# Reordered first loads, pre-gated down weights, a DMA-transposed norm and a new instruction order in an adaLN transformer block

## The chip, the cores and the metric

The kernel runs on one core of one Trainium2 chip. The metric is the device time of one execution in microseconds (us). A run counts as slow when it is over 1.5% above the fastest of the same kernel. The granted clock is TensorE's clock as a share of its full speed; over a stretch it is a mean. Engines are called TensorE (PE in the profile), VectorE (DVE), ScalarE (ACT), GpSimd (POOL) and SyncE (SP), the last of which issues nearly all DMAs here.

## The reference, cut to what matters

A block with adaptive layer norm: 2048 tokens, width 448, 16 heads of 28, a dilated local window of 8 keys (distance 2), and a gated feed-forward part with 1792 hidden columns.

```python
mod = (silu(c) @ w_mod).reshape(...)           # six rows of 448: sa, ca, ga, sb, cb, gb
h = layernorm(x) * (1 + ca) + sa
x = x + ga * attention(h, A_wqkv, A_wo)        # local window, 8 keys
h = layernorm(x) * (1 + cb) + sb
gate = h @ W_gate; up = h @ W_up
h = relu(gate) * up
x = x + gb * (h @ W_down)
```

## The kernel before

The kernel records some 900 operations with their dependencies, estimated costs and priorities. A list scheduler in the kernel's own Python then fixes, before anything is compiled, the order of instructions on every engine. Tokens are handled in four blocks of 512 (b = 0 to 3), in tiles of 128. hT is the normalized block, transposed; the V projection makes v from it and the QK projections make q and k. PSUM is the memory that TensorE writes (psF and psL in the profile), and an eviction copies a result out of it. The parts that the change and the argument touch:

```python
# first loads: x tiles 0-1 and then c on ScalarE's queue, the rest on SyncE's
load_x(0, 2, -9, eng=ACTE)
load(crow[:], c..., ["crow"], 4096, -9, eng=ACTE)
for i, (k0, k1) in enumerate(PARTS_A):
    load(wmod[...], ["wmodA" + str(i)], ...)       # modulation weights for the first norm
    if i == 0:
        load_x(2, 4, -8)
...
load(Wd[:], B_W_down..., [("Wd", f) ...], FF * D * 2, -1)   # 1.57 MB, last of the loads

# first norm of a block by TensorE: normalize -> 16 transposes into PSUM ->
# four evictions that apply scale and shift (two on ScalarE, two on VectorE)
def stage_a_pe(b, prio, groups): ...
# the same by GpSimd and DMA transposes; in the source before, but used for no block (DMAT = ())
def stage_a_dma(b, prio, groups): ...

# output tile of the down stage: PSUM * gate, + x, store
def stage_out(t, buf, eng, eprio):
    o = _Buf(o_slots)
    op(DVE, 620, ... o = buf * gbc[:, 1, :])
    op(eng, ..., ... o = o + x_sb[:, t, :])        # VectorE in the last block, else GpSimd
    op(SP, 0, ... store o)
```

The softmax here doesn't subtract the row's maximum and nothing guards it: scores larger than these inputs give would overflow.

Of the kernel before, what the change touches and what calls it, by code (L numbers as in the profile page):

```python
# [6 lines left out]
ALU = mybir.AluOpType  # L7
# [3 lines left out]
D = 448  # L11
# [4 lines left out]
NF = FF // 128  # L16
NB = 4
# [6 lines left out]
EPS = 1e-5  # L24
DN64 = (1, 2)
PR = {
    "ln1": [537, 334, 2613, 2241],
    "qk": [711, 1230, 2349, 2507],
    "qke": [2263, 2215, -826, -631],
    "v": [2180, 2636, 348, 408, 1319, 433, 2040, 2244, -1257],  # L30
    "at": [374, 331, 536, 709, -821, 2168, 1026, -349, -365, 591, 241, 236, 1043, 1920, 2533, -19, 2605, 2025],
    "ae": [-692, 650, -783, 337, -1128, -747, 13, -538, 1769, -29, 6, 739, 473, 2242, 453, 1030, -831, 2496],
    "y": [-360, 506, 1780, 457, 2055, -380, 840, 939],
    "ye": [2666, -18, 1084, 2214, 693, 151, -437, 215],
    "ln2": [2233, 536, -825, 351],
    "gu": [562, 2728, -159, 2532],
    "dn": [882, 2869, 674, 2816],
    "ffe": [331, 1314, 632, 2250],
    "misc": [2507, 2310, 2251, 237],
}  # L40
T32 = 5
DMAT = ()
SWAP_DVE = (0,)
ACT_TABLE_LN_EXP = 6

# [21 lines left out]


class _Plan:
    SWITCH = 105.0  # L70
    XLAT = 95.0
    DMA_FIXED = 2000.0
    DMA_NS_PER_BYTE = 1.0 / 255.0

# [40 lines left out]
    def schedule(self):  # L115
# [39 lines left out]
        for _ in range(n):  # L155
            cands = {e: [] for e in ENGINES}
            for oid in avail:
                o = ops[oid]
                slot_t = 0.0
                bad = False  # L160
                taken = set()
                for b in o["allocs"]:
                    s = slot_for(b, taken)
                    if s is None:
                        bad = True
                        break
                    taken.add((id(b.slots), s[1]))
                    slot_t = max(slot_t, s[0])
                if bad:
                    continue  # L170
                best = None
                for a, (e, c, f) in enumerate(o["alts"]):
                    rt = slot_t
                    for d in o["deps"]:
                        if d in o["after"]:
                            t = finish[d] + 40.0
                        elif e == PE and who[d] == PE:
                            t = finish[d] - ops[d]["drain"]
                        else:
                            t = finish[d] + lat(d, e)  # L180
                        if t > rt:
                            rt = t
                    st = max(free[e] + (self.SWITCH if e == PE and o["mode"] != mode else 0.0), rt)
                    if e == DVE and o["port"]:
                        st = max(st, free[POOL])
                    elif e == POOL and not o["dma"] and port is not None:
                        st = max(st, finish[port])
                    if best is None or st + c < best[0] - 1e-6:
                        best = (st + c, st, a, e)
                cands[best[3]].append((best[1], o["prio"], oid, best[2]))  # L190
            pick = None
            for e in ENGINES:
                cl = cands[e]
                if not cl:
                    continue
                tmin = min(c[0] for c in cl)
                sel = min((c for c in cl if c[0] <= tmin + slack[e]), key=lambda c: (c[1], c[2]))
                if pick is None or sel[0] < pick[0]:
                    pick = (sel[0], e, sel[2], sel[3])
            if pick is None:  # L200
                raise RuntimeError("static scheduler: dependency cycle")
            st, e, oid, a = pick
            o = ops[oid]
            o["eng"], cost, o["fn"] = o["alts"][a]
            for b in o["allocs"]:
                t, i = slot_for(b)
                prev = b.slots.last[i]
                if prev is not None:
                    o["deps"].update(prev.users)
                b.slots.last[i] = b  # L210
                b.i = i
            if o["dma"]:
                free[e] = st + o["issue"]
                b0 = max(free[e], dma_free)
                dma_free = b0 + o["dma"] * self.DMA_NS_PER_BYTE
                finish[oid] = dma_free + self.DMA_FIXED
            else:
                free[e] = st + cost
                finish[oid] = free[e] + o["drain"]
                if e == POOL and port is not None:  # L220
                    o["deps"].add(port)
                if e == DVE and o["port"]:
                    port = oid
            o["st"] = st
            if e == PE:
                mode = o["mode"]
            who[oid] = e
            order[e].append(oid)
            commit.append(oid)
            avail.remove(oid)  # L230
            for s in succ[oid]:
                left[s] -= 1
                if left[s] == 0:
                    avail.append(s)
# [61 lines left out]


def _mm(n):
    return max(n, 60) / 2.4 + 3.0


def _act(n, ptr=0):
# [3 lines left out]
def _dve(n, per=1.04, fixed=150.0, ptr=0):  # L306
    return fixed + per * n + 90.0 * ptr


PE_DRAIN = 175.0  # L310


def bass_adaLN_cond__sliding_local_dilated__glu_gated_reglu__prompt_kernel(
# [15 lines left out]
    with ExitStack() as es:  # L329
# [121 lines left out]

        PARTS_A = ((0, 2), (2, 3), (3, 4))
        wmod_v = w_mod.rearrange("(p k) n -> p k n", k=4)
        load_x(0, 2, -9, eng=ACTE)
        load(crow[:], c.rearrange("o (p k) -> (o p) k", k=4), ["crow"], 4096, -9, eng=ACTE)
        for i, (k0, k1) in enumerate(PARTS_A):
            load(wmod[0:112, k0:k1, 0:2 * D], wmod_v[:, k0:k1, 0:2 * D], ["wmodA" + str(i)], (k1 - k0) * D * D, -8)
            if i == 0:
                load_x(2, 4, -8)
        load(Wv[:, 0:3, :], A_wqkv[0:384, 2 * D:3 * D].rearrange("(k p) n -> p k n", p=128),  # L460
# [138 lines left out]
        def stage_a_pe(b, prio, groups):  # L599
# [21 lines left out]
            for j in range(4):  # L621
                hbufs.append(ln_normalize(t0 + j, rstd, nmr, 1, prio, ((0, 1), (0, 1, 2), (2,), (2,))[b]))
                if b == 0:
                    op(PE, 4 * 64, lambda e, j=j: tr(e, (j,)), r=[hbufs[j], "ident"], w=pairs[2 * (j // 2):2 * (j // 2) + 2] + [("tr", b, j)], prio=prio,
                       drain=PE_DRAIN)
                    if j < 3:
                        keep_busy(1, prio, 300, [("tr", b, j)])
            if b:
                op(PE, 16 * 64, lambda e: tr(e, range(4)), r=hbufs + ["ident"], w=pairs + [("tr", b, 3)], prio=prio,
                   drain=PE_DRAIN)  # L630
            for h in range(1 if b else 2):
                for cc in range(4):
# [253 lines left out]
                   r=[bufs[1], gs] + ([hh] if f else []), w=[(hh, f)] + ([] if f else [hh] + extra), prio=eprio)  # L886
            return hh

        def stage_out(t, buf, eng, eprio):
            o = _Buf(o_slots)  # L890
            op(DVE, 620, lambda e: e.tensor_tensor(o.at, buf.at[:, 0:D], gbc[:, 1, :], ALU.mult), r=[buf, ("gbc", 1)], w=[o],  # L891
               prio=eprio)
            op(eng, 400 if eng == DVE else 1030, lambda e: e.tensor_tensor(o.at, o.at, x_sb[:, t, :], ALU.add), r=[o, ("x", t)],  # L893
               w=[(o, "x")], prio=eprio, port=eng == DVE)
            op(SP, 0, lambda e: e.dma_start(out2d[128 * t:128 * t + 128, :], o.at), r=[o, (o, "x")], w=[("out", t)], prio=0,
               dma=128 * D * 2)
# [25 lines left out]

        def stage_down1(b, hh, prio, eprio):
            for j in range(4):
                buf = _Buf(poolF if b == NB - 1 else poolM)
                for part in range(2):
                    def mm(e, j=j, buf=buf, part=part):
                        last = None
                        for f in range(7 * part, 7 * part + 7):
                            last = e.matmul(buf.at[:, 0:D], hh.at[:, f, 128 * j:128 * j + 128], Wd[:, f, :],  # L930
                                            start=(f == 0), stop=(f == NF - 1))
                        return last
                    op(PE, 7 * _mm(D), mm, r=[hh] + [(hh, f) for f in range(7 * part, 7 * part + 7)] +
                       [("Wd", f) for f in range(7 * part, 7 * part + 7)], w=[buf], prio=prio, drain=PE_DRAIN)
                t = 4 * b + j
                stage_out(t, buf, DVE if b == NB - 1 else POOL, eprio)


        mod_cols((0, 1), "wmodA", 0, -5, PARTS_A)
# [28 lines left out]
        for t in range(NA):  # L968
            stage_attn(t, PR["at"][t], PR["ae"][t])
            end = sum(span(t)[:2])  # L970
            while done_y < NT and 128 * (done_y + 2) <= end:
                stage_y(done_y, PR["y"][done_y // 2], PR["ye"][done_y // 2])
                done_y += 2
                if done_y % 4 == 0:
                    h2s.append(stage_ln2(done_y // 4 - 1, PR["ln2"][done_y // 4 - 1]))
        for b in range(NB):
            hh = stage_gu(b, h2s[b], PR["gu"][b], PR["ffe"][b])
            (stage_down if b in DN64 else stage_down1)(b, hh, PR["dn"][b], PR["ffe"][b])

# [53 lines left out]
```

## Time and profile before

224.74 us (median of 3 runs, 224.7 to 225.2). The first lines of the page of the kernel before: span, busy time with its share and the number of instructions, then the busy tenths in 40 slices of 5.6 us.

```profile
span 222.2 us, 5740 instructions
PE 212.7 (96%) x2452; PEld 102.7 (46%) x2452; DVE 143.3 (65%) x299; ACT 119.5 (54%) x210; POOL 49.1 (22%) x73
...
PE   7699999989999999999999999999999999999992
...
DVE  2889999888879967842387659569444304544251
ACT  2658799989879697340286676822333301433200
POOL 7402450310220020028302001281660005100000
...
DMA  6999999900130030021302000240440001100011
```

TensorE is busy nearly everywhere, but "busy" hides slow stretches: until about the tenth slice VectorE and ScalarE are nearly full as well, because they empty PSUM for TensorE and run the softmax. Loads fill the DMA engines through the eighth slice. Waits, by stretch and by engine (each line of waits: who waited for whom, us in total, times, longest; the stretch line: length, then busy us of TensorE, its weight loads, VectorE, ScalarE, GpSimd, then granted clock, DMA share, GB/s):

```profile
ACT cexp L490 <- DMA crow<-in_c_dram: 4.9, 1, 4.9
PE psF L507 <- DVE silu L493: 1.7, 1, 1.7
```

```profile
30.00:40.00 10.00, 9.56 (x178) 4.86 (x175) 9.70 (x20) 9.73 (x17) 1.71 (x3) 1.00 1.04 231
```

The time can be cut into three pieces at two landmarks: the start of the first V projection (the first useful large matmul) and the first matmul of the last down stage. The timeline of the kernel before (start, length, what, count):

```profile
11.58 3.30 PE L724 MATMUL psF<-Wv,hT 64*128 64x448 bf16 x28
...
217.89 0.62 DVE L891 TENSOR_TENSOR o_sb<-psF,gbc 128x448 bf16<-128x448 f32 x1 [1.53 <-PE psF L930]
218.55 0.39 DVE L893 TENSOR_TENSOR o_sb<-o_sb,x_sb 128x448 bf16<-128x448 bf16 x1
```

The last down stage starts at 207.09 us. So the start takes 11.58, the middle 195.51 and the tail 15.11 us.

### The profile page before, as it was taken

The page shows a single profiled execution, that of the slowest core. Times are in us where ns is not written, and L with a number is a line of the kernel's source. Part 1 is how long each engine was busy: PE and PEld are TensorE (multiplying, and loading weights), DVE is VectorE, ACT ScalarE, POOL GpSimd, SP SyncE. Part 2 cuts the span into 40 slices and gives each one's busy share as a digit, 9 for nine tenths or more (in the row PEclk, how much of TensorE's full clock was granted, in tenths as well). Part 3 has the DMA queues.
Part 4 walks back from the last instruction along what each step waited for, and adds up shares of the span by engine and source line. Part 5 has one row for each costly group of instructions (what it writes and reads, how often), then busy time and mean ns, then how long its engine had stood idle before and what let it go on. Part 6 is the DMA issues. An engine that isn't in the chain of part 4 may idle for free.

```text
span 222.2 us, 5740 instructions
## 1 busy us (share of the span) xinstructions
PE 212.7 (96%) x2452; PEld 102.7 (46%) x2452; DVE 143.3 (65%) x299; ACT 119.5 (54%) x210; POOL 49.1 (22%) x73
## 2 busy tenths in 40 slices
PE   7699999989999999999999999999999999999992
PEld 3344345555534445445544455554444454444450
DVE  2889999888879967842387659569444304544251
ACT  2658799989879697340286676822333301433200
POOL 7402450310220020028302001281660005100000
PEclk9999999999999999999999999999999999999999
DMA  6999999900130030021302000240440001100011
GB/s 174 334 274 237 200 229 238 274 5 3 27 71 3 0 52 3 0 52 41 103 24 47 3 3 1 50 96 31 91 109 21 3 0 41 44 0 3 1 41 43
DMA packets 19634, 16.52 MB, mean 74 GB/s; under 512 B 9624, under 2 KB 17880, under 8 KB 19608
## 3 DMA queue, kind: packets, MB, share of 16 engines
q1 hardware_dynamic: 19208, 15.92, 29.6%
q8 instruction: 19, 0.31, 0.6%
q10 hardware_dynamic: 400, 0.23, 0.4%
q14 instruction: 7, 0.06, 0.1%
HBM read 10.84 MB, written 1.84 MB: 57 GB/s over the span
## 4 chain that ended last, share of the span: by engine, by line
PE 87%; DVE 4%; ACT 3%; DMA 3%; issue 1%
PE psF L875 29%; PE psF L681 10%; PE psF L930 10%; PE psF L912 10%; PE psF L877 9%; PE psF L724 6%; PE psF L832 6%; PE psL L763 3%; DMA crow<-in_c_dram 3%; PE psF L796 2%; PE psF L808 1%; PE psF L619 1%; ACT EA L776 1%; DVE qT L696 1%; DVE EA L782 1%
## 5 line engine op out<-in xcount | busy, mean ns | idle before, releaser
L877 PE MATMUL psF<-h2T,Wgu 64*128 64x512 bf16 x392 | 87.7, 376 | 0.0
L875 PE MATMUL psF<-h2T,Wgu 64*128 64x512 bf16 x392 | 87.7, 376 | 0.0
L883 ACT ACTIVATE g_sb<-psF 128x512 bf16<-128x512 f32 x56 | 33.4, 597 | 52.8 <-PE psF L877 52.5
L885 DVE TENSOR_TENSOR bigR<-psF,g_sb 128x512 bf16<-128x512 f32 x56 | 38.6, 690 | 30.4 <-ACT g_sb L883 30.2
L875 PEld LDWEIGHTS psF<-h2T,Wgu 64*128 64x128 bf16 x392 | 36.2, 94 | 33.8 <-DVE st L538 0.2
L877 PEld LDWEIGHTS psF<-h2T,Wgu 64*128 64x128 bf16 x392 | 36.2, 94 | 9.8
L776 ACT ACTIVATE EA<-psL 128x912 bf16<-128x912 f32 (+1 forms) x36 | 33.3, 925 | 12.6 <-PE psL L763 12.5
L556 POOL TENSOR_SCALAR hb<-x_sb,rstd,nmr 128x448 bf16<-128x448 bf16 x22 | 15.5, 716 | 87.2 <-DVE nmr L549 81.5
L681 PE MATMUL psF<-hT,Wqk 64*128 64x512 bf16 x224 | 27.9, 377 | 0.5 <-ACT kT L703 0.2
L782 DVE TENSOR_TENSOR EA<-EA,maskA 128x912 bf16<-128x912 bf16 (+1 forms) x36 | 23.1, 646 | 6.6 <-ACT EA L776 6.1
L891 DVE TENSOR_TENSOR o_sb<-psF,gbc 128x448 bf16<-128x448 f32 x16 | 9.7, 622 | 22.7 <-PE psF L930 13.2
L912 PE MATMUL psF<-Wd,bigR 64*128 64x448 bf16 x224 | 22.5, 349 | 0.0
L538 DVE BATCH_NORM_STATS2 st<-x_sb 128x6 f32<-128x448 bf16 x32 | 19.7, 614 | 3.1 <-DMA x_sb<-in_A_x_dram 2.8
L930 PE MATMUL psF<-Wd,bigR 128*128 128x448 bf16 x112 | 21.5, 353 | 0.0
L893 POOL TENSOR_TENSOR o_sb<-o_sb,x_sb 128x448 bf16<-128x448 bf16 x12 | 12.2, 1031 | 26.3 <-DVE o_sb L891 26.3
L681 PEld LDWEIGHTS psF<-hT,Wqk 64*128 64x128 bf16 x224 | 9.6, 94 | 13.3 <-PE psF L681 2.8
L930 PEld LDWEIGHTS psF<-Wd,bigR 128*128 128x128 bf16 x112 | 10.8, 98 | 10.4 <-issue 0.4
L912 PEld LDWEIGHTS psF<-Wd,bigR 64*128 64x128 bf16 x224 | 10.8, 94 | 9.9
L832 PE MATMUL psF<-wo_pad,qT 64*128 64x448 bf16 x128 | 14.6, 350 | 0.6 <-DVE qT L818 0.5
L724 PE MATMUL psF<-Wv,hT 64*128 64x448 bf16 x126 | 14.2, 352 | 0.3
L572 POOL TENSOR_SCALAR h2T<-h2T,modc 128x512 bf16<-128x512 bf16 (+1 forms) x14 | 11.0, 797 | 13.4 <-DMA h2T<-hb 13.4
L818 DVE TENSOR_TENSOR qT<-psF,lnD 128x456 bf16<-128x456 f32 (+1 forms) x18 | 11.3, 627 | 2.2 <-ACT lnD L816 2.1
(75 smaller groups left out, 212.9 us busy)
## 6 DMA issues: line engine op xcount, KB each, us to landing
out_dram<-o_sb SPq DMA_DIRECT2D x16, 112.0 KB, 1.7
Wd<-in_B_W_down_dram SPq DMA_DIRECT2D x1, 1568.0 KB, 26.5
x_sb<-in_A_x_dram SPq DMA_DIRECT2D x3, 448.0 KB, 9.3
Wgu<-in_B_W_gate_dram SPq DMA_DIRECT2D x3, 448.0 KB, 17.5
Wgu<-in_B_W_up_dram SPq DMA_DIRECT2D x3, 448.0 KB, 19.5
bigR<-in_w_mod_dram SPq DMA_DIRECT2D x1, 1176.0 KB, 15.5
bigR<-in_w_mod_dram SPq DMA_DIRECT2D x2, 392.0 KB, 6.7
h2T<-h2T SPq DMA_DIRECT2D x3, 256.0 KB, 3.1
```

The costliest lines, as they stand in the source:

```text
L538: op(DVE, 613, lambda e: e.bn_stats(stt[:, t, :], x_sb[:, t, :]), r=[("x", t)] + list(extra), w=[(tag, "st", t)], prio=prio)
L681: last = e.matmul(bufs[sec].at, Wqk[h0:h0 + 64, k, c0:c0 + 128], hT[h0:h0 + 64, k, KOFF + TB * b:KOFF + TB * b + TB], start=(phase == 0 an ...
L724: last = e.matmul(bufs[i].at[0:nk, 0:D], hT[h0:h0 + 64, k, KOFF + k0:KOFF + k0 + nk], Wv[h0:h0 + 64, k, :], start=(phase == 0 and n == 0), ...
L776: return e.activation(dst, src, ACT.Exp)
L782: return e.tensor_tensor(d, d, msk[0:nk, None, 0:nq].to_broadcast([nk, 8, nq]), ALU.mult)
L832: last = e.matmul(bufs[i].at[:, 0:D], qT[h0:h0 + 64, g, s0:s0 + 128], wo_pad[h0:h0 + 64, g, :], start=(phase == 0 and g == 0), stop=(phase ...
L875: e.matmul(bufs[0].at, Wgu[0:64, c, 128 * f:128 * f + 128], h2.at[0:64, kg, :], start=(c == 0), stop=(c == 6))
L877: last = e.matmul(bufs[1].at, Wgu[64:128, c, 128 * f:128 * f + 128], h2.at[64:128, ku, :], start=(c == 0), stop=(c == 6))
L883: op(ACTE, _act(TB), lambda e, gs=gs, gb=bufs[0]: e.activation(gs.at, gb.at, ACT.Relu), r=[bufs[0]], w=[gs], prio=eprio)
L885: op(DVE, _dve(TB), lambda e, gs=gs, ub=bufs[1], f=f: e.tensor_tensor(hh.at[:, f, :], ub.at, gs.at, ALU.mult), r=[bufs[1], gs] + ([hh] if ...
L912: last = e.matmul(bufs[i].at[:, 0:D], hh.at[rows[i], f, 128 * (j + i):128 * (j + i) + 128], Wd[rows[i], f, :], start=(phase == 0 and f == ...
L930: last = e.matmul(buf.at[:, 0:D], hh.at[:, f, 128 * j:128 * j + 128], Wd[:, f, :], start=(f == 0), stop=(f == NF - 1))
```

## The change

Four things change. (1) c is loaded alone on ScalarE's queue, x tiles 0-1 move to the head of SyncE's queue, and the scheduler is told the true size of the first modulation loads. (2) Block 3's first norm uses `stage_a_dma`: GpSimd normalizes, DMA transposes, GpSimd applies scale and shift; 16 TensorE transposes and four PSUM evictions go. (3) Before the last down stage GpSimd multiplies the 14 slices of the down weights by the output gate, so that each output tile there needs one addition; the last tile is computed in two halves of 224 columns. (4) All priorities and some costs of the scheduler are new, so nearly every engine's order is new.

```diff
-    "ln1": [537, 334, 2613, 2241],
... (all 13 lists of priorities are replaced)
+    "ln1": [2543, -183, 2164, 2302],
-DMAT = ()
+DMAT = (3,)
-    SWITCH = 105.0
-    XLAT = 95.0
+    SWITCH = 95.0
+    XLAT = 80.0
+    OVERLAP = {PE: 0.0, ACTE: 85.0, DVE: 75.0, POOL: 40.0, SP: 0.0}
... (further costs of the scheduler)
-        load_x(0, 2, -9, eng=ACTE)
         load(crow[:], c.rearrange("o (p k) -> (o p) k", k=4), ["crow"], 4096, -9, eng=ACTE)
+        load_x(0, 2, -9)
...
+                scaled = b == NB - 1
+                cols = ((0, D // 2), (D // 2, D)) if scaled and j == 3 else ((0, D),)
...
+                    if scaled:
+                        op(DVE, _dve(n1 - n0), lambda e, ...: e.tensor_tensor(
+                            o.at[:, n0:n1], buf.at[:, 0:n1 - n0], x_sb[:, t, n0:n1], ALU.add), ...)
...
         for b in range(NB):
+            if b == NB - 1:
+                for f in range(NF):
+                    op(POOL, 1030, lambda e, f=f: e.tensor_tensor(Wd[:, f, :], Wd[:, f, :], gbc[:, 1, :], ALU.mult),
+                       r=[("Wd", f), ("gbc", 1)], w=[("Wd", f)], prio=3000, port=True)
```

## The prediction

> **What bounds the kernel now.** The page's first part gives TensorE 212.7 us busy in a span of 222.2 us, at the full clock. By the timeline of TensorE, useful matmuls start at 11.58 us (first V projection) and end at about 217.8 us: 206.3 us. Counting 512 columns as 0.213 us and 448 as 0.187 us (spacing in the saturated later stages), the same matmuls need about 197 us. The rest is stalls. After 60 us groups run at nominal spacing. Between 15 and 58 us they do not (QK 1.85 instead of 1.49 us, last transposes 1.61 instead of 1.0). There the busy time by stretch shows VectorE 9.70 and ScalarE 9.73 of 10 us (30 to 40 us). So three parts can shrink: the start, the evictions before 58 us, and the tail.
>
> **Costs, from the trace.**
> 1. Start. The table of waits puts 4.9 us of ScalarE on the load of c (landed 6.91) and 1.7 us of TensorE on silu; x tiles 0-1 landed at 5.49. After: c is alone on ScalarE's queue, x is first on SP's. c should land about 2 us earlier, and the silu chain no longer splits the statistics on VectorE. [...] First V matmul 0.7 to 1 us earlier; I count -0.8.
> 2. Last token block's norm. Removes 16 TensorE transposes (1.0 us, 1.6 with their stall), two ScalarE evictions (0.72 each) and two of VectorE (0.5 each). Adds 8 GpSimd normalizations in place of 4 of 0.72, 4 DMA transposes (about 1.25 us issue, 2.5 us to landing), and 4 GpSimd affines (0.75 to 0.85). On the path: -1.0 on TensorE, about -0.5 through fewer evictions.
> 3. Last down stage. Adds 14 GpSimd multiplies of about 1.03 us (14.4 us), between the end of the third down stage (about 186 us) and the last one (207 us): with four output additions 18.5 us of 21, off the path. Removes 4 VectorE multiplies; the final eviction shrinks from 0.62 + 0.39 us to one half-width addition of about 0.38: -0.65. Splitting the last tile into 28 matmuls of 224 columns costs at most 0.15.
> 4. New priorities: about as many changes of tile shape (64 against 65), the last QK block moved before the gate/up stage. About 0, perhaps -0.5.
>
> **Sum** 224.7 - 0.8 - 1.5 - 0.6 - 0.1 = 221.7 us; range 219.8 to 223.9. Chances: faster by over 2% 0.15, within 2% 0.82, slower by over 2% 0.03.
>
> **What would show each step.** (1) First V projection at 10.5 to 11 us; c no longer the longest wait of ScalarE. (2) The transpose group has 48 matmuls; V and QK groups between 15 and 58 us closer to nominal. (3) GpSimd gating ends by about 203 us and no TensorE wait names it; span end minus last matmul falls from 4.4 to about 3.7 us. (4) TensorE busy throughout after 60 us.
>
> **What would make it wrong.** The four DMA transposes stand behind the 1.57 MB down-weight load in SP's queue (issued 19.2, landing 45.7 us). If they land near 50 us,[...] the last block's V projection (due at about 52 us) waits: +1 to 3 us. The new order could create PSUM waits between 20 and 60 us, or remove most of the 4 to 5 us of stalls there (then under 220).

224.7 less 0.8, 1.5, 0.6 and 0.1 is 221.7 us. Its 197 us of matmuls is the author's estimate, from spacings of 0.213 and 0.187 us; in the trace of the kernel before, a pair of matmuls of 512 columns follows the last pair after 0.216 us (gate and up stages) and one of 448 columns after 0.189 (down stages), so the estimate is some 2 us low. The 0.15 us for the halves of the last tile is an estimate that no trace stood behind.

## The result, and the profile after

221.28 us (median of 4 runs, 220.84 to 221.72) against 224.78 us: a ratio of 0.984 (95% interval 0.9816 to 0.9864), so 1.6% faster. A ratio here is the mean time of one kernel's fast runs over the mean of the other's fast runs of the same rounds, so it is not quite the ratio of the medians. 221.7 us, 219.8 to 223.9, was forecast.

The changed kernel's page, the lines that answer to those above:

```profile
span 219.9 us, 5739 instructions
PE 210.9 (96%) x2450; PEld 104.2 (47%) x2450; DVE 139.5 (63%) x292; ACT 116.8 (53%) x208; POOL 69.4 (32%) x97
...
PE   7999799799999999999999999999999999999993
...
DVE  5779787788999997743266594556574303554331
ACT  2849999878887799751067234433343302334200
POOL 7407560434021211500330013530502505997000
...
DMA  6999999950240202200110004130003220100011
```

GpSimd carries 20 us more. TensorE has two new dips, in the fifth and the eighth slice. Waits of the changed kernel, and its timeline at the landmarks, at the transposes and in the tail:

```profile
ACT cexp L491 <- DMA crow<-in_c_dram: 1.3, 1, 1.3
PE psF L725 <- ACT hT L642: 1.4, 2, 1.2
PE psL L764 <- issue: 1.3, 1, 1.3
PE psL L764 <- DVE hT L697: 0.5, 1, 0.5
```

```profile
10.32 3.31 PE L725 MATMUL psF<-Wv,hT 64*128 64x448 bf16 x28 [0.20 <-ACT hT L642]
...
30.61 15.98 SPq L567 DMA_TRANSPOSE hT<-hb  x4
47.95 3.03 POOL L596 TENSOR_SCALAR hT<-hT,modc 128x512 bf16<-128x512 bf16 x4 [2.58 <-DMA hT<-hb]
...
185.86 4.01 POOL L992 TENSOR_TENSOR Wd<-Wd,gbc 128x448 bf16<-128x448 bf16 x4
189.82 2.03 POOL L894 TENSOR_TENSOR o_sb<-o_sb,x_sb 128x448 bf16<-128x448 bf16 x2
191.80 9.96 POOL L992 TENSOR_TENSOR Wd<-Wd,gbc 128x448 bf16<-128x448 bf16 x10
...
216.19 0.39 DVE L942 TENSOR_TENSOR o_sb<-psF,x_sb 128x224 bf16<-128x224 f32 x1 [0.95 <-PE psF L936]
```

The start shrank by 1.26 us. c landed at 3.3 us instead of 6.9. The tail shrank by 0.56 us: two serial operations of 0.62 and 0.39 us became one of 0.39. The gating ended at 201.8 us, before the last down stage (205.35). The middle took 195.03 us, only 0.48 less. The line of DMA transposes shows that issuing four of them stretched over 16 us: SyncE was busy with the first issue alone for 9.74 us, against a median of 1.26 us for the 16 transposes issued later, and that transpose landed 14.0 us after its start, at 44.6 us, just after the down weights (44.1 us). The last block's hT was ready at 51.0 us, and the first V projection that needs it starts at 53.3 us, so nobody waited.

Executions differ by 0.5 us and more, so I profiled the changed program three times, and two kernels with the old order, which differ from before in one piece only. Pieces in us, from the timelines:

| profile | start | middle | tail | span |
|---|---|---|---|---|
| before | 11.58 | 195.51 | 15.11 | 222.2 |
| old order, new loads (b_start) | 10.28 | 196.11 | 15.11 | 221.5 |
| old order, new tail (b_tail) | 11.62 | 196.08 | 14.50 | 222.2 |
| changed | 10.32 | 195.03 | 14.55 | 219.9 |
| changed again (a_same) | 10.66 | 195.33 | 14.51 | 220.5 |
| changed again (a_ref) | 10.36 | 194.80 | 14.54 | 219.7 |

The span is printed to 0.1 us, so a tail here is good to about 0.05 us.

Means of the pieces that are alike: the start fell from 11.60 to 10.45 (or 10.40 with b_start), the middle from 195.90 to 195.05, the tail from 15.11 to 14.53: 1.15 + 0.85 + 0.58 = 2.6 us. The timed difference was 3.5 us in the first timing. By the ratios, it was 1.1% (a_same) and 1.35% (a_ref) of about 225 us in two later ones, 2.6 and 3.0 us. The profiled single executions agree with the smaller of these.

### The profile page after: what moved, and what is told of

It reads as the page before. It is cut to its first block, busy times and chain, and to the rows that moved or that the text cites. A ratio compares the mean times of both kernels' runs of the same rounds, so it can differ in the third digit from the quotient of the medians.

```text
span 219.9 us, 5739 instructions
## 1 busy us (share of the span) xinstructions
PE 210.9 (96%) x2450; PEld 104.2 (47%) x2450; DVE 139.5 (63%) x292; ACT 116.8 (53%) x208; POOL 69.4 (32%) x97
## 3 DMA queue, kind: packets, MB, share of 16 engines
HBM read 10.84 MB, written 1.84 MB: 58 GB/s over the span
## 4 chain that ended last, share of the span: by engine, by line
PE 90%; ACT 4%; DVE 2%; DMA 1%; issue 1%
PE psF L876 37%; PE psF L682 11%; PE psF L936 10%; PE psF L913 10%; PE psF L833 6%; PE psF L725 6%; PE psL L764 4%; PE psF L797 3%; PE psF L878 2%; PE psF L809 2%; DMA crow<-in_c_dram 1%; ACT hT L642 1%; PE psF L529 1%; ACT hb L559 1%; ACT qT L695 1%
## 5 line engine op out<-in xcount | busy, mean ns | idle before, releaser
L886 DVE TENSOR_TENSOR bigR<-psF,g_sb 128x512 bf16<-128x512 f32 x56 | 38.6, 689 | 41.5 <-ACT g_sb L884 41.2
L783 DVE TENSOR_TENSOR EA<-EA,maskA 128x912 bf16<-128x912 bf16 (+1 forms) x36 | 24.5, 684 | 8.8 <-ACT EA L777 7.7
L682 PE MATMUL psF<-hT,Wqk 64*128 64x512 bf16 x224 | 26.8, 377 | 0.0
L894 POOL TENSOR_TENSOR o_sb<-o_sb,x_sb 128x448 bf16<-128x448 bf16 x12 | 12.3, 1035 | 30.7 <-DVE o_sb L892 30.1
L936 PE MATMUL psF<-Wd,bigR 128*128 128x448 bf16 (+1 forms) x126 | 21.6, 332 | 0.0
L539 DVE BATCH_NORM_STATS2 st<-x_sb 128x6 f32<-128x448 bf16 x32 | 18.5, 609 | 0.0
L936 PEld LDWEIGHTS psF<-Wd,bigR 128*128 128x128 bf16 x126 | 12.1, 98 | 9.6 <-issue 0.8
L573 POOL TENSOR_SCALAR h2T<-h2T,modc 128x512 bf16<-128x512 bf16 (+1 forms) x13 | 9.9, 772 | 19.7 <-DMA h2T<-hb 10.0
L725 PE MATMUL psF<-Wv,hT 64*128 64x448 bf16 (+1 forms) x126 | 14.3, 351 | 1.5 <-ACT hT L642 1.4
L764 PE MATMUL psL<-qT,kT 64*128 64x114 bf16 (+6 forms) x208 | 12.4, 205 | 2.1 <-issue 1.3
L992 POOL TENSOR_TENSOR Wd<-Wd,gbc 128x448 bf16<-128x448 bf16 x14 | 14.0, 1041 | 0.0
(78 smaller groups left out, 224.6 us busy)
```

Of the source, the lines that this page charges most:

```text
L682: last = e.matmul(bufs[sec].at, Wqk[h0:h0 + 64, k, c0:c0 + 128], hT[h0:h0 + 64, k, KOFF + TB * b:KOFF + TB * b + TB], start=(phase == 0 an ...
L725: last = e.matmul(bufs[i].at[0:nk, 0:D], hT[h0:h0 + 64, k, KOFF + k0:KOFF + k0 + nk], Wv[h0:h0 + 64, k, :], start=(phase == 0 and n == 0), ...
L764: last = e.matmul(buf.at[0:nk, i, n * NQ + o:n * NQ + o + w], kT[rows, g, KOFF + k0:KOFF + k0 + nk], a, start=True, stop=True)
L783: return e.tensor_tensor(d, d, msk[0:nk, None, 0:nq].to_broadcast([nk, 8, nq]), ALU.mult)
L886: op(DVE, _dve(TB), lambda e, gs=gs, ub=bufs[1], f=f: e.tensor_tensor(hh.at[:, f, :], ub.at, gs.at, ALU.mult), r=[bufs[1], gs] + ([hh] if ...
L936: last = e.matmul(buf.at[:, 0:n1 - n0], hh.at[:, f, 128 * j:128 * j + 128], Wd[:, f, n0:n1], start=(f == 0), stop=(f == NF - 1))
```

## The experiments

Changing one line of this kernel lets its scheduler reshuffle everything, which would mix the effect of the line with that of a new order. So I recorded the order of both kernels and replayed it. Every operation that a variant shares with its base kept its engine and its place among the shared operations of that engine; only added operations were placed by the scheduler. Replayed without an edit, the changed kernel came out instruction for instruction the same (a_same). For the kernel before no unedited replay was run, but in the trace of b_start every engine has the order of before, and only the moved load differs. Line numbers in the variants' profiles differ, because the recorded order stands at their top; the names of tiles tell what a line is. All twelve variants gave correct results. Each batch of four ran on one chip beside the kernel before; ratios are to that.

### First batch: one part at a time in the old order, and the new order without the parts

`b_start`, `b_tail`, `b_dmat` apply part 1, 3 or 2 to the kernel before. `a_none` is the changed kernel with parts 1, 2 and 3 undone and the new order kept.

```diff
# b_start
-        load_x(0, 2, -9, eng=ACTE)
         load(crow[:], ..., eng=ACTE)
+        load_x(0, 2, -9)
# b_tail
+            if b == NB - 1: ... 14 multiplies of Wd by gbc[:, 1, :] on POOL
+            one addition per output tile of the last block, last tile in two halves
# b_dmat
-DMAT = ()
+DMAT = (3,)
# a_none: the three edits reversed in the changed kernel
```

> The kernel before in its own order of instructions on every engine, with only the first loads changed: c alone on ScalarE's queue, x tiles 0-1 first on SP's. Theory A (the parts of the change add up, each on its own): the first V projection starts near 10.3 us instead of 11.6, and the time falls by about 1.2 us, to 223.5. Rival B (the head start is eaten by the evictions that fill VectorE and ScalarE until 58 us): the start moves as much, but the time falls by 0.4 us or less.

Measured: 223.09 us against 224.02, ratio 0.9944 (0.9918 to 0.9970). The first V projection began at 10.28 us. So 1.30 us of start gave 0.9 us (medians) to 1.25 us (ratio): theory A, the head start survives. Two loads moved at once: c landed at 3.1 us instead of 6.9, and x tiles 0-1 at 3.7 us instead of 5.5. No run tells their shares apart.

> The kernel before in its own order, with only the down weights pre-gated on GpSimd before the last down stage, one addition per output tile there, and the last tile in two halves. Theory A: 0.6 us less, to 224.2, all of it after the first matmul of the last down stage, whose TensorE time does not grow by more than 0.15. Rival B: the 14 multiplies on GpSimd hold up VectorE or the output additions, and the gate/up stage of the last block grows by as much as the tail gains: 224.8.

Measured: 223.70 us, ratio 0.9978 (0.9951 to 1.0005). The tail piece fell from 15.11 to 14.50 us, as in the changed kernel (14.51 to 14.55), and the middle was that of b_start (196.08 and 196.11). That is more than the 195.51 of before; both have a gap of 0.4 us of TensorE, told of below, that before does not have. The timed difference alone does not clear zero, the piece in the trace does.

> The kernel before in its own order, with only the first norm of the last token block moved to GpSimd and DMA transposes. Theory A (the prediction's term, independent of the order): 1.5 us less, to 223.3. Rival B (the move needs the new order): before transposes the last block at 39.8 us and runs its V projections (tiles 14 to 17) from 43.6 us, while transposes in SP's queue land only behind the down weights, at 45 to 48 us, and the affines end near 51 us; TensorE then waits 5 to 7 us at that V projection and the time rises to 228 to 231 us.

Measured: 234.03 us, ratio 1.0431 (1.0399 to 1.0464): 10 us slower, worse than even theory B's range. The waits of TensorE, the timeline at that place (first in the kernel before, then in b_dmat), and two stretches (the granted clock is the third number from the end):

```profile
PE psF L1012 <- POOL hT L883: 7.1, 1, 7.1
PE psL L1051 <- ACT kT L991: 1.2, 1, 1.2
```

```profile
43.57 0.97 PE L724 MATMUL psF<-Wv,hT 64*128 64x448 bf16 x8
50.67 1.75 PE L1012 MATMUL psF<-Wv,hT 64*128 64x448 bf16 x8 [7.15 <-POOL hT L883]
```

```profile
50.60:53.00 2.40, 2.33 (x20) 1.82 (x22) 0.00 (x0) 0.00 (x0) 0.71 (x2) 0.50 0.00 0
53.00:56.00 3.00, 2.94 (x36) 0.99 (x32) 2.03 (x4) 1.44 (x2) 0.00 (x0) 0.78 0.00 0
```

V projections of the last block stand at 43.6 us in the old order, and hT came at 50.6. After the wait TensorE ran at half clock: eight matmuls took 1.75 us that take 0.97 in the kernel before. The trace has 7.15 us of wait, then a clock of 0.50, and 1.00 again from 54.3 us, 3.6 us after the wait ended. So theory A, which was my prediction's term, is wrong as it was put: in the old order the move saves nothing, it costs.

> The new order of instructions on every engine, with the three parts undone (loads as before, down weights not pre-gated, last block transposed on TensorE where the scheduler puts it). Theory A (order is worth little by itself): 224.3 to 224.8 us. Rival B (the order is the larger part of the gain): 223.3 us or less.

Measured: 228.62 us, ratio 1.0195 (1.0159 to 1.0232). Neither theory: the new order without the parts is 2% slower. Its first V projection began at 13.55 us, and TensorE's clock was 0.71 between 12 and 16 us. The new order is neither a gain of its own nor neutral; it pays with the parts.

### Second batch: one part taken away from the changed kernel

The edits reverse part 1, 2 or 3 in the changed kernel, with its order replayed; `a_same` has no edit.

```diff
# a_nostart
-        load_x(0, 2, -9)
+        load_x(0, 2, -9, eng=ACTE)      # again ahead of c
# a_nodmat
-DMAT = (3,)
+DMAT = ()
# a_notail: multiply and add for each tile again, no gating, no halves
```

> The changed kernel, instruction for instruction, built through the recorded order: a second profile and a control of that method. 221.0 to 221.6 us. The gap of 1.3 us at 41.5 us, in which TensorE waits for nothing in the middle of one group, is either in this profile too (a property of the program) or gone or elsewhere (an accident of the profiled execution[...]).

Measured: 222.48 us against 224.83, ratio 0.9886 (0.9837 to 0.9934), with a wide spread: four runs at a clock of 1.00 took 220.9 to 222.6 us, two at 0.991 and 0.992 took 223.9 and 224.6 (one of these counted as slow). The gap came back at the same instruction. Here are the two profiles, changed first, then a_same (the bracket is TensorE's idle time before the row):

```profile
41.28 0.22 PE L764 MATMUL psL<-qT,kT 28*128 28x56 bf16 x2 [0.22 <-ACT EA L777]
42.81 0.38 PE L764 MATMUL psL<-qT,kT 28*128 28x56 bf16 x14 [1.30 <-issue]
```

```profile
42.61 0.22 PE L1071 MATMUL psL<-qT,kT 28*128 28x56 bf16 x2 [0.22 <-ACT EA L1084]
43.45 0.38 PE L1071 MATMUL psL<-qT,kT 28*128 28x56 bf16 x14 [0.61 <-issue]
```

It is a property of the program, not an accident: two of 16 matmuls of one group run, then TensorE stands still though the profile shows no wait for a semaphore. In every profile that has the gap, and I looked at eight, it ends 2.4 to 2.7 us after a packet on the queue that the profile calls "instruction" (found by narrowing the window of the DMA view: packet at 40.40 and end at 42.81 in the changed kernel, 40.95 and 43.45 in a_same, 39.65 and 42.34 in b_start).

Counting the matmuls of all fourteen traces tells more. In all eight profiles with the gap, in the old order and in the new one, it stands before the 472nd or 473rd matmul that the trace lists, although in the two orders (b_start and b_tail against the others) these are matmuls of different groups. In the six profiles without a gap that matmul starts 2.5 us or more after the packet anyway: 2.5 us in a_nostart, 2.9 us in the kernel before, 3.4 to 10.8 us in the others. So in no trace does it start earlier than 2.36 us after the packet. In the changed kernel that queue has 19 packets, and the packet in question is the third. What a packet carries the profile does not say.

> The changed kernel in its own order, with only the first loads put back (x tiles 0-1 and then c on ScalarE's queue). Theory A (parts add up): the loss equals what the loads gave the old order, 0.9 us, so 222.2. Theory B (loads and order were tuned together): the new order runs the silu chain on VectorE before the first statistics, so everything on VectorE waits for c at 6.9 us, the first V projection starts near 13.5 us instead of 10.3 (as in the run with the order alone), and the time rises by 2.5 to 3.2 us, to about 224.

Measured: 224.65 us, ratio 0.9993 (0.9957 to 1.0028). Set against a_same's 0.9886 of the same chip, the loads are worth 1.1% or 2.4 us in the new order, and 1.25 us in the old one. The cause is as theory B says. In the profile VectorE waits 4.58 us before the first operation on c and starts its first statistics only at 7.76 us, though x tiles 0-1 had landed at 5.9; in the changed kernel they start at 4.19.

```profile
7.27 0.17 DVE L799 TENSOR_SCALAR cexp<-cexp 112x4 f32<-112x4 f32 x1 [4.58 <-ACT cexp L798]
...
7.76 1.14 DVE L846 BATCH_NORM_STATS2 st<-x_sb 128x6 f32<-128x448 bf16 x2
```

The first V projection began at 14.11 us instead of 10.32. TensorE also ran at a clock of 0.79 between 12 and 16 us, and all six executions have a mean clock of 0.991 or 0.992.

> The changed kernel in its own order, with only the last token block's first norm put back to TensorE transposes, placed by the scheduler ahead of their first use. Theory A (the prediction's term): 1.5 us slower, 222.8. Theory B (the new order leaves no room for it: transposes and their evictions on a full ScalarE and VectorE meet the last V projections): 3 us slower or more, with a wait of TensorE for the evictions of hT of 1.5 us or more near 54 us.

Measured: 224.35 us, ratio 0.9977 (0.9938 to 1.0017; one run of 229.6 us is not in it). Against a_same that is 0.9% or 2.0 us. TensorE ran the 16 transposes at 52.87 us and then waited for ScalarE's two evictions:

```profile
55.78 0.93 PE L1032 MATMUL psF<-Wv,hT 64*128 64x448 bf16 x8 [1.84 <-ACT hT L949]
```

1.07 us of transposes and 1.84 of wait: closer to theory B's 3 us in the trace, between the theories in time. In the new order the DMA path gains more than I had put down for it: 2.2 us by the middle piece (197.5 against 195.33). The timed difference alone, with an interval of about 1.4 us on each side, would not show that.

> The changed kernel in its own order, with only the last down stage put back (no pre-gated weights, multiply and add for each tile, no halves). The tail is independent of the order: 0.5 to 0.6 us slower, 221.8, the difference all after the start of the last down stage. Rival: the gating on GpSimd costs something before, and putting it back gains there: 221.3.

Measured: 223.68 us, ratio 0.9921 (0.9871 to 0.9972), so 0.35% or 0.8 us above a_same. But its runs fall into two groups: 221.3 and 221.5 us at a clock of 1.00, 223.6 to 224.1 at 0.989 to 0.992. The profiled one is of the second group. Its stretches around the gap:

```profile
39.74:43.15 3.41, 1.61 (x32) 1.23 (x30) 2.91 (x6) 2.57 (x5) 1.87 (x3) 1.00 1.64 314
43.20:46.50 3.30, 3.24 (x30) 1.17 (x28) 0.63 (x1) 1.60 (x2) 0.79 (x2) 0.50 0.95 105
46.60:50.00 3.40, 3.40 (x68) 1.77 (x68) 2.96 (x6) 2.01 (x4) 0.52 (x1) 1.00 0.21 40
```

Here the gap was 1.58 us, and after it the clock was 0.50 for 3.4 us. The executions at a clock of 1.00 are no slower than those of a_same at that clock (220.9 to 222.6), so the timed 0.8 us lies in the low-clock executions and doesn't show what the tail is worth. For the tail I trust its own piece: 15.15 us in this profile, 14.51 in a_same, a difference of 0.64 us. The rival (gating costs something) finds no support there: the multiplication of gate and up on VectorE, which runs beside the gating, had a mean of 689 ns after and 690 before. The 14 gating multiplies took 1037 to 1049 ns each, about as long as GpSimd's 12 additions of the same size in the kernel before (mean 1031).

### Third batch: the place in the queue, the gap, and an attempt to do better

```diff
# a_wdlate: the changed kernel; b_dmat_wdlate: b_dmat
-        load(Wd[:], ..., FF * D * 2, -1)                       # behind the other loads
+        load(Wd[:], ..., FF * D * 2, -1, r=[("hTr", 15)])      # after the fourth new transpose has landed
# a_better: a_wdlate, and in the recorded order
#   TensorE: 16 transposes of block 1 ahead of the last phase of QK of block 0;
#   their four evictions ahead of the last q and k evictions of block 0 (ScalarE)
#   and of the next statistics (VectorE)
```

> The changed kernel itself again, as the reference on this chip for the three runs beside it: 0.982 to 0.989 of before. If the gap of TensorE near 42 us belongs to the program's place in time[...], it appears again within 1 us of the same place, 2.4 to 2.7 us after an instruction packet that lands near 40.5 us, as in five profiles so far.

Measured: 221.41 us against 224.99, ratio 0.9865 (0.9823 to 0.9906). The gap appeared at the same instruction, 0.76 us long, ending 2.6 us after an instruction packet.

> The changed kernel with the 1.57 MB load of the down weights issued only after the four new transposes have landed, nothing else moved. The first down stage needs them near 100 us, so nothing waits for them. Theory F[...]: with the DMA engines idle from about 39 us the gap is gone, and the time falls by 0.6 to 1.5 us against the changed kernel of this batch. Rival: the gap stays[...], and the time is within 0.3 us.

Measured: 220.73 us (220.16 to 220.94), ratio 0.9816 (0.9791 to 0.9841). It is the fastest kernel, and its interval lies well under 1. Against the changed kernel beside it, it is 0.7 us lower by the medians, but the two intervals overlap a little, so that step is likely and not proven. Theory F, that the gap comes of the loads in flight, fell: the gap is still there, at the same instruction.

```profile
41.32 0.22 PE L1069 MATMUL psL<-qT,kT 28*128 28x56 bf16 x2 [0.23 <-ACT EA L1082]
42.08 0.38 PE L1069 MATMUL psL<-qT,kT 28*128 28x56 bf16 x14 [0.54 <-issue]
```

It ended 2.5 us after its instruction packet, just as with full queues; the DMA share from 39.60 to 42.10 us was 0.00. What the middle gained (194.27 against 194.80 in a_ref) is the shorter gap (0.54 against 0.76) and a wait of 0.26 us of the second gate row for its weights, which this profile does not have; that wait was 0.93 us in a_same and absent in the first profile of the changed kernel. The last transpose landed at 46.9 us instead of 47.8 (a_ref); nothing on TensorE had waited for it.

> The kernel before in its own order, with the last block's first norm on DMA transposes, as in the run that lost 10 us, but with the load of the down weights issued after them. If that loss was the place in the queue behind the loads: transposes land near 40 us instead of 47.5, the affines end near 44 us, TensorE's wait of 7.1 us falls under 1 us, and the time is 222.5 to 225. If it was the transposes or the GpSimd work themselves, 230 us or more.

Measured: 229.79 us, ratio 1.0229 (1.0203 to 1.0256). That is halfway: of 4.3% lost in b_dmat, 2.0 come from the down weights ahead in the queue. The waits fell from 7.15 to 3.91 us, and hT was still late, because the gate and up weights, still ahead in the queue, landed only at 41.5 us, and the four transposes at 41.9, 43.8, 44.3 and 44.7:

```profile
47.90 1.00 PE L1010 MATMUL psF<-Wv,hT 64*128 64x448 bf16 x4 [3.91 <-POOL hT L881]
```

My expectation of 40 us was too hopeful. I had taken 2.5 us from issue to landing for each, but even the first landed 12.3 us after its issue. The clock was again 0.50 after the wait (50.6 to 53.0 us). The place in the queue shows: the last of the same four transposes landed 2.8 us earlier (44.7 instead of 47.5) when 1.57 MB less stood before them.

> The changed kernel with the down weights loaded late as above and, against the wait of 1.2 us before the V projection at 23.4 us, the 16 transposes of the second token block moved ahead of the last phase of the first QK block, its four evictions ahead of that block's last q and k evictions. If the wait is on the path, the third V projection starts near 22.5 us and the time is 0.5 to 1 us under the run with the late load alone; if VectorE and ScalarE bind there until 42 us, it is within 0.3 us of it.

Measured: 222.69 us, ratio 0.9903 (0.9876 to 0.9930): 2 us slower than a_wdlate. The wait was not removed but split: the transposes themselves now waited 0.79 us for ScalarE's eviction of q, and the third V projection 0.79 us for hT, and it started at 23.81 us, no earlier. The gap near 42 us was gone from this profile (the group started 4.3 us after its packet), and the kernel still lost. Neither expectation came out: the time was to be 0.5 to 1 us lower or the same. That the wait moved to ScalarE's eviction of q fits ScalarE and VectorE binding there, but a run that lost 2 us doesn't show it. What else the reordering disturbed I did not trace.

## Why the prediction was right, and where it was right by luck

The sum held: 221.7 forecast, 221.28 measured. The terms did not hold equally.

1. **Start.** Forecast -0.8 us and a first V projection at 10.5 to 11 us. Measured 10.32 to 10.66, and -1.15 us in the mean of the profiles. c landed 3.6 us earlier and not 2: its load no longer stood behind x tiles 0-1 on the same queue (2.5 us from issue to landing instead of 5.7). Taken alone it gave 0.9 to 1.25 us. The mechanism fits and the term was too small; how much of it is c and how much the earlier x tiles stays open.

2. **Last block's norm.** Forecast -1.0 us of transposes and -0.5 of evictions, as a saving that stands by itself. As a step this is wrong. In the old order it costs 10 us (b_dmat), because the last block's V projections stood at 43.6 us and the transposes landed only when the loads ahead of them had (44.7 to 47.5 us). I saw that queue and gave it 1 to 3 us as a risk, but I asked only whether the new order would wait. I also misread the old timeline: the transposes at 48.12 us, which I called the last block's, are block 2's; the recorded order shows that block 3 came first, at 39.77 us. In the new order the move is worth about 2.0 us: putting it back brings 1.07 us of transposes and 1.84 us of wait.

3. **Tail.** Forecast -0.6 us; 15.11 fell to 14.53 us. The gating ended at 201.8 us, forecast by about 203. The halves of the last tile cost nothing that the trace shows: the matmuls of the stage took 10.80 us from 205.35, against 10.8 (207.09 to the eviction at 217.89) before. From the last matmul to the end of the span it is 3.7 us, as forecast, against 4.4 before. This term was right in mechanism and size; gating and halves were not tested apart.

4. **Order.** Forecast "about 0, perhaps -0.5" for the new priorities. Alone they cost 2% (a_none). Parts 1 and 2 and the order are one design: the new order puts c's chain first on VectorE, which only pays if c lands at 3.3 us, and moves the last block's projections to 53 us, after the DMA transposes have landed (47.9 us). The three losses of taking a part away (2.4, 2.0 and, for the tail, 0.64 us) add to 5.0 us; less the 4.4 us that the order alone costs, the whole would gain 0.6, and it gained about 2.6 on that chip. With intervals of about 1.4 us on two of the losses this alone does not decide. Single parts do: the norm's move costs 10 us in the old order and gains 2.0 in the new; the loads bring the first V projection forward by 1.3 us in the old order (11.58 to 10.28) and by 3.8 in the new (14.11 to 10.32). Start and norm have no worth apart from an order, so they are not terms of a sum; only the tail is the same in both.

5. **The middle.** The prediction expected -1.6 us between the landmarks (terms 2 and 4). The profiles show -0.85. As far as the timelines show, what was saved in transposes and slow groups was partly given back as waits: 1.15 us before the V projection at 23.4 us, for which block 1's hT came late from ScalarE, and the gap of 0.6 to 1.3 us near 42 us (0.4 us in b_start and b_tail). So the start gained 0.35 us more and the middle 0.75 us less than forecast, and the two errors partly cancelled. By the pieces the change is worth 2.6 us, where 3.0 was forecast and 3.5 was timed first. That the sum met the time within 0.5 us was luck in this much: term 2 stood on a misread timeline, and it held only because the new order moved the projections out of the way.

What stays open: why TensorE stands still at that place. The place is a count of matmuls, the same in both orders, and its end follows an instruction packet by 2.4 to 2.7 us, with full and with idle data queues. No run changed that queue alone, so the cause is not shown. Open too is why the mean clock is lower in some executions (4 of 6 of a_notail, 2 of 6 of a_same, none of 6 of a_ref, which is the same program, none of 5 of a_wdlate); these took about 2.5 us longer. Only one of them was profiled, so that the clock fell after the gap in the others too is likely and not shown. What makes the clock fall these runs do not show. In a_notail TensorE was busy for 1.61 of the 3.41 us before the drop to 0.50. In the changed kernel it was busy for 2.25 us of 39.03 to 42.45, and in a_nodmat for 1.57 us of 53.94 to 57.35, and neither had a drop.

## What to carry to other kernels

Before adding up savings, ask of each part which order of the engines it needs and whether the old order has it; a part that helps in one order can cost many times its worth in another. Here data that passed through a queue shared with bulk loads was ready only when the loads ahead of it were done (in the changed kernel the first transpose landed at 44.6 us, just after the down weights at 44.1; in b_dmat the last one landed at 47.5 us, and in b_dmat_wdlate, with 1.57 MB less ahead of it, at 44.7), so its first consumer had to be placed after that moment, or the bulk load behind it. When a scheduler sits in the kernel, replay its recorded order for experiments, and cut the trace into pieces at landmarks, because piece by piece the profiles repeat better than the total time does.
